# Fewer block products for the query, gate and up matmuls of an attention and feed-forward layer: q through DRAM, one unit per 64-row half

## The chip, the cores and the metric

The kernel runs on one core of one Trainium2 chip. The metric is device time in microseconds of one execution, without the launch. Four runs of the kernel before lie within 0.06% (556.2 to 556.51 us). Five engines matter here: PE (TensorE, the matrix unit; its weight loads are listed apart as PEld), DVE (VectorE), ACT (ScalarE), POOL (GpSimd) and SP (SyncE, which here does nothing but issue DMAs). In the traces here each engine works through its own queue in the order in which the program put the instructions there; when the q stores alone left SP's queue (e9_storepool, below), a wait of PE fell from 19.2 to 3.4 us.

## The reference, cut to what matters

```python
# x: 2048 x 448, bf16.  16 query heads of 256, 8 key/value heads, last W = 512 keys
xn = layernorm(x)
q  = xn @ wq                                    # 448 -> 16 x 256
p  = softmax(q @ k[last 512]^T * 256 ** -0.5)   # two query heads share a kv head
s  = (p @ v[last 512]) @ wo                     # 16 x 256 -> 448
g  = silu((gelu(xn @ w_gate) * (xn @ w_up)) @ w_down)   # 448 -> 1792 -> 448
out = x + s * g
```

The contraction of q, gate and up has length 448 = 7 x 64. That is an awkward length for the matmuls of 128 rows that the traces show elsewhere (128*128): three full ones and a half one.

## The kernel before

It computes on tokens in four chunks of 512. Everything between the end of the head and the tail is a queue of matmuls on PE with the other engines behind it. Two outputs of a pair, j = 0 and 1 (gate and up of 128 columns, or the two 128-column halves of a q head), are computed together: one 64-row half of PE works for one output while the other half works for the other, and then they change over (such a pair took 0.2157 us, below).

```python
def group(units, lo, hi, start, stop, phases=(0, 1)):
    for p in phases:
        ...                                     # cut: ks is [2, 1, 0, NK]; NK is the 64-row rest
        for (b, w, wr, cols, reads, rreads, xts) in units:
            for k in ks:
                if k == NK and ph == 1:
                    continue
                for u, j in ((0, ph), (1, 1 - ph)):      # the two 64-row halves, side by side
                    rows = slice(R * u, R * u + R)
                    l = wr[rows] if k == NK else w(j, k)[rows]
                    lst.append((bank[b + j][:, lo:hi], l, xnT[rows, k, cols], ...))
```

So an output costs seven 64-row matmuls of 512 columns, and a pair of outputs takes seven slots of PE. The order of work: all gate and up (112 units of 128 columns by 512 tokens), with the down projections of finished chunks between them; then attention, where q is computed for 8 or 12 heads at a time and kept in SBUF until it is used:

```python
LAG = 2
for m in range(NS):                 # 4 chunks x 16 heads
    if m in groups:                 # q for the next 8 or 12 heads
        for i in range(m, groups[groups.index(m) + 1], 2):
            q_group(i, (cur, nxt)[i // 2 % 2])
    s_mm(m)      # 8 matmuls; exp on ACT into p; DVE scales p into pn;
                 # SP issues two DMA transposes pT <- pn (dma_t)
    if len(late) == LAG:
        pv(late.pop(0))             # 8 matmuls of pT with v
    ...                             # cut: after 16 heads, 64 matmuls with wo for each 256 tokens
    late.append(m)
```

All weights, keys and values lie in SBUF before attention starts: wq, kT, va and wo are loaded from POOL's and SP's queues in the middle of gate and up, when nobody is waiting for them.

The softmax here doesn't subtract the row's maximum and nothing guards it: scores larger than these inputs give would overflow.

Of the kernel before, what the change touches and what calls it, by code (L numbers as in the profile page):

```python
# [8 lines left out]
F32 = mybir.dt.float32  # L9

LN_EPS = 1e-5
P = 128
# [3 lines left out]
class Buf:  # L16
# [3 lines left out]
    __slots__ = ("lo", "hi", "writer", "readers")  # L20

    def __init__(self, lo, hi):
        self.lo, self.hi = lo, hi
        self.writer = None
        self.readers = []

# [10 lines left out]
class Plan:  # L37
# [16 lines left out]
    def buf(self, lo=0, size=0):  # L54
        b = Buf(lo, lo + size)
        self.bufs.append(b)
        return b

    def reuse(self, new):


        for b in new:
            for x in self.bufs:
                if x not in new and x.lo < b.hi and b.lo < x.hi:
                    b.readers.extend(x.readers)
                    if x.writer is not None:
                        b.readers.append(x.writer)

    def op(self, eng, fn, reads=(), writes=(), dma=False, after=()):
        o = Op(eng, fn, dma)  # L70
        raw = {b.writer: None for b in reads if b.writer is not None}
        deps = dict(raw)
        for b in writes:
            if b.writer is not None:
                deps[b.writer] = None
            deps.update((x, None) for x in b.readers)


        for d in deps:
            if d.eng == eng and not d.dma and not dma and (eng == "pe" or d not in raw):  # L80
                continue
            o.deps.append(d)
        o.deps.extend(after)
        for b in writes:
            b.writer, b.readers = o, []
        for b in reads:
            b.readers.append(o)
        self.ops.append(o)
        return o
# [75 lines left out]
def bass_recurrent_scan__sliding_block_cached__geglu_ffn__prompt_kernel(  # L165
# [19 lines left out]
    QC = 512  # L185
# [12 lines left out]
    HG = 8  # L198
    NG = Hq // HG
    QS = 12  # L200

    es = ExitStack()
    with es:
# [3 lines left out]
        def place(name, shape, dt, at=None):  # L207
            size = {BF16: 2, F32: 4}[dt]
# [36 lines left out]
        xnT, a, _ = place("xnT", [P, NK + 1, S], BF16)  # L245
        b_xnT = [[K.buf(), K.buf()] for t in range(NT)]
        g2, a, _ = place("g2", [P, NT, D], BF16)
        b_g2 = sbuf_bufs(a, D * 2, NT)
        kT, a, _ = place("kT", [P, Hkv, 2, W], BF16)
        b_kT = sbuf_bufs(a, 2 * W * 2, Hkv)  # L250
        va, a, _ = place("va", [P, Hkv, NJ, Dh], BF16)
        b_va = [K.buf() for g in range(Hkv)]
        wq, a, _ = place("wq", [P, NK, HD], BF16)
        wqr, a, _ = place("wqr", [P, Hq, P], BF16)
        b_wql = [[K.buf() for i in range(3)] for g in range(NG)]
        NXR = 3
        xr, a, _ = place("xr", [P, NXR, D], BF16)
        b_xr = sbuf_bufs(a, D * 2, NXR)
        ofin, a, _ = place("ofin", [P, 2, D], BF16)
        b_ofin = [[K.buf(a + (i * D + lo) * 2, (hi - lo) * 2) for lo, hi in ((0, CUT), (CUT, D))] for i in range(2)]  # L260
# [3 lines left out]
        rw = base[0]  # L264
        wo, _, rw_end = place("wo", [P, NCO, D], BF16)
        b_wo = sbuf_bufs(rw, 8 * D * 2, NCO // 8)
        x4, a, a2 = place("x4", [P, NT, D], BF16, at=rw)
        b_x4 = sbuf_bufs(a, D * 2, NT)
        NXN = (rw_end - a2) // (DP * 2)
        xn, a, a2 = place("xn", [P, NXN, DP], BF16, at=a2)  # L270
        b_xn = [[K.buf(a + i * DP * 2, D * 2), K.buf(a + i * DP * 2 + D * 2, R * 2)] for i in range(NXN)]
        assert a2 <= rw_end

        rf = base[0]
        wgu, a, at = place("wgu", [P, 2, NK, F], BF16, at=rf)
        wgur, _, at = place("wgur", [P, F], BF16, at=at)
        b_wgu = K.buf(a, at - a)
        FBL = [0, 3, 6, 9, NF]
        b_wl = [[K.buf() for j in range(2)] for i in range(4)]
        b_wlr = [[K.buf() for j in range(2)] for i in range(3)]  # L280
        wd, a, at = place("wd", [P, NF, D], BF16, at=at)
        b_wd = K.buf(a, at - a)
        actT, a, at = place("actT", [P, 2, NF, QC], BF16, at=at)
        b_actT = [sbuf_bufs(a + i * NF * QC * 2, QC * 2, NF) for i in range(2)]
        NGL = 3
        gl, a, at = place("gl", [P, NGL, QC], BF16, at=at)
        b_gl = sbuf_bufs(a, QC * 2, NGL)


        NPT, NPN, NP32 = 3, 3, 3  # L290
        pT, a, at = place("pT", [P, NPT, 2, 2, NJ, P], BF16, at=rf)
        b_pT = [sbuf_bufs(a + i * QC * NJ * 2, QC * NJ, 2) for i in range(NPT)]
        pn, a, at = place("pn", [P, NPN, 2, W], BF16, at=at)
        b_pn = sbuf_bufs(a, 2 * W * 2, NPN)
        p32, a, at = place("p32", [P, NP32, W], F32, at=at)
        b_p32 = sbuf_bufs(a, W * 4, NP32)
        assert at <= b_wgu.hi
        oT, a, at = place("oT", [P, NCO, QC], BF16, at=b_wgu.hi)
        b_oT = sbuf_bufs(a, QC * 2, NCO)
        qT, a, at = place("qT", [P, QS, 2, QC], BF16, at=b_gl[0].lo - (QS - HG) * 2 * QC * 2)  # L300
        assert b_oT[-1].hi <= a
        b_qT = [[K.buf(a + (h * 2 + e) * QC * 2, QC * 2) for e in range(2)] for h in range(QS)]
# [8 lines left out]
        def qs(n):  # L311
            return QS - 1 - n % QS


# [6 lines left out]
        def act(o, i, func, reads, writes, scale=1.0):  # L321
            K.op("act", lambda e, o=o, i=i: e.activation(o, i, func, scale=scale), reads, writes)  # L322
# [167 lines left out]
        def gu_evac(n, b):  # L490
            c, f = divmod(n, NF)
            s = n % NGL
            act(gl[:, s, :], bank[b], ACT.Gelu_apprx_tanh, (b_ps[b],), (b_gl[s],))
            K.op("dve", lambda e: e.tensor_tensor(actT[:, c % 2, f, :], bank[b + 1], gl[:, s, :], ALU.mult),  # L494
                 (b_ps[b + 1], b_gl[s]), (b_actT[c % 2][f],))

        def down(c, pairs):
            for t4 in range(4):
                t = c * 4 + t4
                b = bk(pairs, t4)  # L500
                mms([(bank[b][:, 0:D], actT[:, c % 2, f, t4 * P:(t4 + 1) * P], wd[:, f, :], f == 0, f == NF - 1)
                     for f in range(NF)], [b_wd] + b_actT[c % 2], (b_ps[b],))
                s = t % 2
                act(tmp[:, s, :], bank[b][:, 0:D], ACT.Tanh, (b_ps[b],), b_tmp[s], scale=0.5)
                K.op("dve", lambda e, t=t, b=b, s=s: e.scalar_tensor_tensor(
                    out=g2[:, t, :], in0=tmp[:, s, :], scalar=1.0, in1=bank[b][:, 0:D],
                    op0=ALU.add, op1=ALU.mult), b_tmp[s] + [b_ps[b]], (b_g2[t],))
# [61 lines left out]
        def load_k(g):  # L569
            dma_t(kT[:, g, :, :], A_k_cache[0, g, Sk - W:Sk, :], (), (b_kT[g],))  # L570

        def load_v(g):
            dma("pool", va[:, g, :, :],
                A_v_cache[0, g, Sk - W:Sk, :].rearrange("(j p) d -> p j d", p=P), (), (b_va[g],))

        def load_wq(g):
            lo, hi = g * HG * Dh, (g + 1) * HG * Dh
            dma("pool", wq[:, :, lo:hi], A_wq[0:K3, lo:hi].rearrange("(k p) f -> p k f", p=P), (), (b_wql[g][0],))
            for e in range(2):
                dma("pool", wqr[R * e:R * e + R, g * HG:(g + 1) * HG, :],  # L580
                    A_wq[K3:D, lo:hi].rearrange("p (h e f) -> p h e f", e=2, f=P)[:, :, e, :], (), (b_wql[g][1 + e],))

        DOWN_AT = {NF + 5: 0, 2 * NF + 1: 1}
# [4 lines left out]
        NU = NQC * NF  # L588
        cur, nxt = (0, 2), (4, 6)
        for n in range(4, NU, 2):  # L590
# [4 lines left out]
            if ln_t[0] < 8 or n >= 12:  # L595
# [6 lines left out]
            if n == 32:  # L602
                for g in range(NG):
                    load_wq(g)
                for g in range(Hkv):
                    load_v(g)
                for g in range(Hkv):
                    load_k(g)
                K.reuse(b_wo)
                for i in range(NCO // 8):  # L610
                    dma("pool", wo[:, i * 8:(i + 1) * 8, :],
                        A_wo.rearrange("(c p) d -> p c d", p=P)[:, i * 8:(i + 1) * 8, :], (), (b_wo[i],))
                for t in range(NXR):
                    dma("pool", xr[:, t, :], x_view[:, t, :], (), (b_xr[t],))
            if n + 1 in DOWN_AT:
                down(DOWN_AT[n + 1], cur)
                cur, nxt = nxt, cur


        def q_group(n, pairs):  # L620

            c, h = divmod(n, Hq)
            units = [(b, lambda j, k, i=i: wq[:, k, (h + i) * Dh + j * P:(h + i) * Dh + (j + 1) * P],
                      wqr[:, h + i, :], slice(c * QC, (c + 1) * QC), b_wql[h // HG][:1], b_wql[h // HG][1:], b_xnT[c * 4:c * 4 + 4])
                     for i, b in enumerate(pairs)]
            group(units, 0, QC, True, True)
            for i, b in enumerate(pairs):
                s = qs(n + i)
                act(qT[:, s, 0, :], bank[b], ACT.Copy, (b_ps[b],), (b_qT[s][0],))
                K.op("dve", lambda v, s=s, b=b: v.tensor_copy(qT[:, s, 1, :], bank[b + 1]),  # L630
                     (b_ps[b + 1],), (b_qT[s][1],))

# [161 lines left out]
```

## Time and profile before

| | before |
|---|---|
| time, median of 3 runs | 556.32 us (556.2 to 556.45) |
| span of the profiled run | 554.7 us, granted PE clock 1.00 |
| PE busy | 547.6 us, 99% |
| read from and written to HBM | 17.92 MB, 1.84 MB |

The page's first part gives busy time by engine, the fourth the chain of work that ended last, the fifth the costliest groups of instructions (busy time, mean ns of one, then the idle time before them and who ended it), the sixth the DMAs with the time from issue to landing. Of the kernel before:

```profile
PE 547.6 (99%) x3603; PEld 261.2 (47%) x3628; DVE 317.2 (57%) x817; ACT 273.6 (49%) x727; POOL 32.7 (6%) x64
...
PEclk9999999999999999999999999999999999999999
...
PE 98%; DMA 1%; issue 0%; DVE 0%; SPq 0%; ACT 0%
...
L328 PE MATMUL bank<-xnT,wq 64*128 64x512 bf16 x768 | 94.4, 376 | 0.0
L328 PEld LDWEIGHTS bank<-xnT,wq 64*128 64x128 bf16 x768 | 36.9, 94 | 46.5 <-ACT p L643 2.1
...
L647 DVE TENSOR_SCALAR pn<-p,rden 128x512 bf16<-128x512 f32 x256 | 124.6, 487 | 14.4 <-DMA pT<-pn 5.4
...
pT<-pn SPq DMA_TRANSPOSE x128, 2.8
```

PE is the bound: 98% of the chain is PE's own work, and the weight load of 94 ns is hidden behind the matmul that runs (a slot is 216 ns, below). The row PEclk shows full clock in all 40 slices. PE's list of waits is nearly empty (total us, times, longest us):

```profile
PE bank L445 <- DVE epst L359: 1.2, 1, 1.2
PE bank L328 <- ACT qT L322: 1.0, 6, 0.2
...
```

What a slot costs is read from PE's timeline in gate and up (start, length, and how many matmuls stand in the piece):

```profile
53.71 2.11 PE L328 MATMUL bank<-xnT,wgu 64*128 64x512 bf16 x18
55.65 0.38 PE L328 MATMUL bank<-xnT,wgur 64*128 64x512 bf16 x2
55.87 0.81 PE L328 MATMUL bank<-xnT,wgu 64*128 64x512 bf16 x6
56.52 0.38 PE L328 MATMUL bank<-xnT,wgur 64*128 64x512 bf16 x2
56.73 0.38 PE L328 MATMUL bank<-xnT,wgu 64*128 64x512 bf16 x2
```

From 53.71 to 56.73 there are 28 matmuls, 14 pairs: 0.2157 us for a pair of half-array matmuls. A matmul's own length of 0.38 us is not its cost, because matmuls overlap (the first piece ends at 55.82, the next has begun at 55.65); only the distance between starts counts. With this slot, the stages can be added up from counts: gate and up 84.6 us, down 42.3, q 96.6, scores and values 220.9, output projection 96.6, head and tail about 13: 554 us, which is the span.

One stage has another engine near its limit. In a stretch of score and value matmuls, the sixteen DMA engines are 0.87 busy (last two numbers: granted clock, then DMA share, then GB/s):

```profile
core 0: us, PE busy (x) PEld busy (x) DVE busy (x) ACT busy (x) POOL busy (x), PEclk, DMA share, GB/s
201.00:212.00 11.00, 10.89 (x51) 5.00 (x51) 9.05 (x28) 9.03 (x28) 0.00 (x0) 1.00 0.87 160
```

### The profile page before, as it was taken

To read this page: it belongs to the slowest core of one execution; us is meant where nothing else is said; L and a number is where in the kernel's file an instruction comes from. 1 tells how busy PE (TensorE), PEld (TensorE's weight loads), DVE (VectorE), ACT (ScalarE), POOL (GpSimd) and SP (SyncE) were. 2 spreads that over 40 slices of the span, in tenths; PEclk is the share of its full clock that TensorE was granted. 3 is DMA by queue.
4 is the path that set the end of the run, shared out by engine and by line. 5 is a ranking of instruction groups with operands and counts; after the bars stand their busy time and mean duration, and the time that the engine had idled before them with its cause. 6 is when DMAs were issued, how large, how long until landed. Compare 5 with 4: busy or idle time off the path is not lost.

```text
span 554.7 us, 9719 instructions
## 1 busy us (share of the span) xinstructions
PE 547.6 (99%) x3603; PEld 261.2 (47%) x3628; DVE 317.2 (57%) x817; ACT 273.6 (49%) x727; POOL 32.7 (6%) x64
## 2 busy tenths in 40 slices
PE   8999999999999999999999999999999999999997
PEld 5554444444544444554444444544444454444455
DVE  6673734443385588326588745258747625858722
ACT  5432324353485588205588635058747505758600
POOL 1120580000000000000000000000000000000000
PEclk9999999999999999999999999999999999999999
DMA  9540399901156077413086803157704713618601
GB/s 295 115 141 9 79 302 307 213 1 39 38 134 96 5 149 157 88 35 92 1 153 152 153 1 77 33 94 164 146 11 95 134 34 90 153 19 153 153 8 34
DMA packets 163599, 57.63 MB, mean 104 GB/s; under 512 B 151456, under 2 KB 160672, under 8 KB 163552
## 3 DMA queue, kind: packets, MB, share of 16 engines
q1 hardware_dynamic: 159488, 45.16, 38.8%
q0 software_dynamic: 3296, 11.27, 6.7%
q8 instruction: 29, 0.48, 0.4%
q10 hardware_dynamic: 768, 0.57, 0.3%
q14 instruction: 18, 0.15, 0.1%
HBM read 17.92 MB, written 1.84 MB: 36 GB/s over the span
## 4 chain that ended last, share of the span: by engine, by line
PE 98%; DMA 1%; issue 0%; DVE 0%; SPq 0%; ACT 0%
PE bank L328 98%; DMA x<-in_A_x_dram 1%; SPq L316 0%; DVE stats L375 0%; ACT xnT L322 0%; DVE tmp L681 0%; ACT ve L391 0%; DVE ofin L684 0%; PE bank L426 0%; DVE mv L378 0%
## 5 line engine op out<-in xcount | busy, mean ns | idle before, releaser
L643 ACT ACTIVATE p<-bank 128x512 f32<-128x512 f32 x256 | 149.2, 597 | 103.3 <-PE bank L328 101.4
L647 DVE TENSOR_SCALAR pn<-p,rden 128x512 bf16<-128x512 f32 x256 | 124.6, 487 | 14.4 <-DMA pT<-pn 5.4
L328 PE MATMUL bank<-pT,va 128*128 128x512 bf16 x512 | 120.8, 379 | 0.0
L328 PE MATMUL bank<-kT,qT 128*128 128x512 bf16 x487 | 117.8, 379 | 2.0 <-ACT qT L322 1.0
L328 PE MATMUL bank<-wo,oT 128*128 128x448 bf16 (+2 forms) x544 | 97.7, 341 | 0.0
L328 PE MATMUL bank<-xnT,wq 64*128 64x512 bf16 x768 | 94.4, 376 | 0.0
L328 PE MATMUL bank<-xnT,wgu 64*128 64x512 bf16 (+2 forms) x768 | 83.9, 350 | 0.4 <-ACT xnT L322 0.4
L328 PEld LDWEIGHTS bank<-pT,va 128*128 128x128 bf16 x512 | 50.1, 98 | 60.4 <-DMA pT<-pn 0.2
L328 PEld LDWEIGHTS bank<-kT,qT 128*128 128x128 bf16 x512 | 49.6, 98 | 61.3 <-issue 2.5
L328 PEld LDWEIGHTS bank<-wo,oT 128*128 128x128 bf16 x544 | 52.0, 98 | 45.5
L630 DVE CAST qT<-bank 128x512 bf16<-128x512 f32 x64 | 42.9, 692 | 51.9 <-PE bank L328 51.9
L322 ACT ACTIVATE qT<-bank 128x512 bf16<-128x512 f32 x64 | 38.2, 597 | 60.7 <-PE bank L328 59.1
L328 PEld LDWEIGHTS bank<-xnT,wq 64*128 64x128 bf16 x768 | 36.9, 94 | 46.5 <-ACT p L643 2.1
L322 ACT ACTIVATE gl<-bank 128x512 bf16<-128x512 f32 x56 | 33.2, 597 | 49.4 <-PE bank L328 46.2
L494 DVE TENSOR_TENSOR actT<-bank,gl 128x512 bf16<-128x512 f32 x56 | 37.8, 689 | 33.4 <-PE bank L328 26.6
L328 PEld LDWEIGHTS bank<-xnT,wgu 64*128 64x128 bf16 x768 | 36.9, 94 | 37.4 <-issue 0.7
L643 ACT ACTIVATION_READ_ACCUMULATOR p<-bank 128x1 f32 x256 | 52.8, 206 | 0.0
L646 DVE RECIPROCAL rden<-rsum 128x1 f32<-128x1 f32 x256 | 40.4, 158 | 20.6 <-ACT p L643 20.0
L681 DVE SCALAR_TENSOR_TENSOR tmp<-bank,g 128x448 f32<-128x448 f32 (+2 forms) x17 | 10.1, 597 | 72.5 <-PE bank L328 72.5
L666 DVE CAST oT<-bank 128x512 bf16<-128x512 f32 x64 | 43.8, 684 | 6.9 <-PE bank L328 6.9
L328 PE MATMUL bank<-wd,actT 128*128 128x448 bf16 x224 | 43.0, 353 | 0.0
L322 ACT ACTIVATE oT<-bank 128x512 bf16<-128x512 f32 x64 | 39.1, 611 | 7.0 <-PE bank L328 7.0
(39 smaller groups left out, 182.9 us busy)
## 6 DMA issues: line engine op xcount, KB each, us to landing
wo<-in_A_wo_dram POOLq DMA_DIRECT2D x4, 896.0 KB, 19.0
wq<-in_A_wq_dram POOLq DMA_DIRECT2D x2, 1536.0 KB, 10.0
va<-in_A_v_cache_dram POOLq DMA_DIRECT2D x8, 256.0 KB, 13.9
pT<-pn SPq DMA_TRANSPOSE x128, 2.8
xr<-in_A_x_dram POOLq DMA_DIRECT2D x16, 112.0 KB, 2.3
out_dram<-ofin SPq DMA_DIRECT2D x15, 112.0 KB, 1.7
wd<-in_B_w_down_dram SPq DMA_DIRECT2D x1, 1568.0 KB, 7.6
x<-in_A_x_dram SPq DMA_DIRECT2D x2, 448.0 KB, 4.4
```

The lines of the kernel that those rows point to most:

```text
L322: K.op("act", lambda e, o=o, i=i: e.activation(o, i, func, scale=scale), reads, writes)
L328: ins = e.matmul(o, lhsT=l, rhs=r, start=st, stop=sp)
L494: K.op("dve", lambda e: e.tensor_tensor(actT[:, c % 2, f, :], bank[b + 1], gl[:, s, :], ALU.mult), (b_ps[b + 1], b_gl[s]), (b_actT[c % 2][ ...
L630: K.op("dve", lambda v, s=s, b=b: v.tensor_copy(qT[:, s, 1, :], bank[b + 1]), (b_ps[b + 1],), (b_qT[s][1],))
L643: K.op("act", lambda e, b=b, r=r, z=z: e.activation(p32[:, z, :], bank[b], ACT.Exp, scale=att_scale, accum_out=rsum[:, r:r + 1]), (b_ps[b] ...
L646: K.op("dve", lambda e, r=r: e.reciprocal(rden[:, r:r + 1], rsum[:, r:r + 1]), (b_rsum[r],), (b_rden[r],))
L647: K.op("dve", lambda e, r=r, z=z, y=y, t=t4 % 2: e.tensor_scalar(pn[:, y, t, :], p32[:, z, :], rden[:, r:r + 1], None, op0=ALU.mult), (b_p ...
L666: K.op("dve", lambda v, i=i, b=b: v.tensor_copy(oT[:, i, :], bank[b]), (b_ps[b],), (b_oT[i],))
L681: K.op("dve", lambda e: e.scalar_tensor_tensor(out=tmp[:, s, c0:c1], in0=bank[b][:, c0:c1], scalar=0.5, in1=g2[:, t, c0:c1], op0=ALU.mult, ...
```

## The change

The intent is to do less on PE. A product of 2 x 2 blocks normally needs eight block products; the well-known trick of Strassen and Winograd does it with seven, for the price of sums of blocks before and after. Here the four output blocks are two outputs by two token chunks, and the contraction of 384 rows is split into two parts of 3 x 64; the last 64 rows are handled apart. A set of four output blocks costs 7 x 3 + 4 = 25 half-array matmuls where it cost 28. The form is used for all of q and for half of gate and up: 23 jobs of two sets, one set on each 64-row half of PE. (The first half of gate and up stays plain: the "plain stage" below. The stage of the 23 jobs, with nine down tiles between them, is the "product stage".)

```python
# 25 matmuls per half; * has 4-byte operands
"P1" 3, "P6"* 3, "P5"* 3, "P3"* 3, "P2" 3, "P7"* 3, "P4"* 3, L12, L11, L22, "Ld"*
```

What had to be added for it, cut from the diff:

```diff
+        def xf_ops(p):        # sums of token blocks, on POOL, results 4 bytes wide
+                    (1.16, lambda ...: pool_tt(x[:, 0, k, :], y, z, ALU.add, ...)),   # and 3 more, and a cast
+        def w_ops(i, js):     # sums of weight blocks, on POOL: 6 operations for a job's set
+        def load_wu(i, kind, n):      # 12 DMAs of 64 x 3 x 128 or smaller for gate/up, 6 for q
+                        dma("sp", dst, src, (), ...)
+        xnO[o, :, cs] <- xnT[i, 0:NK, cs]        # a copy of xn with its halves exchanged, by DMA
...
+        def q_sink(n, p):     # q does not stay in SBUF
+                    stores[m] = task("sp", 0.1, 2.5, lambda: dma("sp", qd[m], qo[:, O[i].i, :, :]...
...
+                ready = [task("sp", 0.8, 4.0, lambda ...: load_wu(WU.i, kind, n), base - 3 * PER, (), [WU])]
+        for g in range(Hkv):          # keys and values only after the last use of xf[1]
+            task("sp", 0.2, 3.0, lambda g=g: dma("sp", va[:, g, :, :], ...), ..., last_p1)
+            task("sp", 0.2, 3.0, lambda g=g: dma_t(kT[:, g, :, :], ...), ..., last_p1)
+        run_schedule(pools, {"pe": 0.0, "act": 1.0, "dve": 1.5, "pool": 2.0, "sp": 0.0})
...
-        LAG = 2
+        LAG = 3
+        for i in range(NCO // 8):     # wo only now: its memory was xnT's and xnO's
+            dma("pool", wo[:, i * 8:(i + 1) * 8, :], ...)
         for m in range(NS):
             s_mm(m)
+            load_q("pool", m + QS)    # 256 KB from DRAM, 8 heads ahead
```

The order in which each engine gets its instructions in the product stage comes from a small scheduler in the kernel itself (`run_schedule`), which plays the stage with assumed durations (the first number of each `task` in the diff, in us). And because in the kernel's layout the 4-byte sums lie where keys and values go, and xnT and xnO where wo goes, keys, values and wo can be loaded only when the product stage ends, and q has to go out to DRAM and come back.

## The prediction

> **What bounds the kernel now.** TensorE. The page's busy row has PE at 99% of a 554.7 us span at clock 1.00; the chain of waits is 98% PE. In the timeline two 64x512 matmuls on the two 64-row halves run side by side, a pair in 0.2157 us (14 pairs, 53.71 to 56.73); a 128x512 matmul takes the same, a 128x448 one 0.189 (128 in 24.2). Sum: gate and up 392 pairs, 84.6; down 224, 42.3; q 448 pairs, 96.6; scores and values 1024, 220.9; output projection 512, 96.6; with 10 us of head and 3 of tail 554, the span. Only PE work or PE waits move it.
>
> **Removed.** 28 half-array matmuls (two outputs x two token chunks x seven 64-row pieces) become 25: seven products of three, and four for the last 64 rows; for half of gate and up (196 pairs) and all q (448): 644 pairs become 575. At 0.2157 us that is 14.9 us, all on the critical path.
>
> **Added.**
> 1. 16 of the 25 have 4-byte operands. The bf16 weight load takes 94 ns (by-form groups) and hides. [...] no trace here shows a 4-byte load. The new kernel's scheduler counts 0.227 us per such slot, so I expect a load just at the limit: 11 ns x 23 x 16 slots, 4 us back. Matmuls I expect at 216 ns, one pass.
> 2. Per gate/up job (two units, 5.4 to 5.6 us of PE) 10 ACT operations at about 0.53 = 5.3 us and 8 DVE at 0.69 = 5.5 us: full, with down tiles as slack; q jobs about 75%. POOL makes the weight sums; its wide work isn't in the trace. Expected PE waits 2 us (at most 5), most in the first seven jobs.
> 3. DMA: q makes 16.8 MB out and in. In score/value stretches DMA is already 0.87 busy (windows, 201 to 212) from two pT transposes per head of 3.45 us. A q load is 128 rows of 2 KB; the trace's 2048-byte packets take 86 ns, so 0.7 us of all 16 engines[...]: 3.7 us per head against 3.45. Lag 3 gives pT one head more, but pn has three buffers. The 3.7 MB wo load now falls on attention's start. Expected PE waits 1 us (at most 5).
>
> Attention's PE work is unchanged and ACT needs about 2.9 of 3.45 us per head: it stays PE-bound.
>
> **Sum.** 556.3 - 14.9 + 4 + 2 + 1 = 548.4. Predicted 548 us, range 541.5 to 558. Faster by over 2%: 0.27, within 2%: 0.63, slower by over 2%: 0.10.
>
> **What would show it.** 23 jobs of two units, 5.4 to 5.6 us each; the 4-byte load near 200 ns[...]; PE idle in all under 10 us, released by ACT, DVE or POOL in the fast stage and pT or pn in attention; pT landing at 3 to 5 us, not 2.8; heads still 3.45 us apart.
>
> **What would make it wrong.** [...] A 4-byte matmul of more than one pass. POOL far slower than planned. DMA saturating so that heads take 3.7 us (over 10 us lost). Or hidden loads and no stalls: 541.

The cuts are statements that no trace or run of this case shows. No term of the sum is among them: it came to 556.3 - 14.9 + 4 + 2 + 1 = 548.4. The 4 us are the author's estimate, from the 0.227 us that the new kernel's scheduler assumes for a slot with a 4-byte load, less the measured 0.2157.

## The result and the profile after

| | before | after |
|---|---|---|
| time, median of 4 runs each | 556.38 us | 615.48 us |
| lowest to highest | 556.2 to 556.51 | 615.17 to 616.34 |
| span of the profiled run | 554.7 us, clock 1.00 | 613.4 us, clock 0.969 |
| PE busy | 547.6 us, 99% | 560.8 us, 91% |
| HBM read, written | 17.92, 1.84 MB | 38.83, 18.61 MB |

The changed kernel is slower: ratio 1.1065, 95% interval 1.105 to 1.1081. A ratio here and below is the mean time of one kernel's fast runs over that of the other's of the same rounds, so it is not quite the ratio of the medians quoted beside it. The outputs were judged correct.

The page after:

```profile
PE 560.8 (91%) x3490; PEld 318.3 (52%) x3518; DVE 359.8 (59%) x882; ACT 335.0 (55%) x847; POOL 161.5 (26%) x227
...
PEclk9998969999999999589899999999999999999999
...
PE 64%; DMA 14%; SPq 7%; DVE 6%; POOL 3%; ACT 3%; issue 2%; DVEq 0%; ACTq 0%; POOLq 0%
...
L746 PE MATMUL bank<-xf,wf 64*128 64x512 f32 x690 | 144.7, 453 | 28.5 <-DVE qo L770 19.2
L1178 DVE TENSOR_SCALAR pn<-p,rden 128x512 bf16<-128x512 f32 x256 | 124.7, 487 | 60.5 <-DMA pT<-pn 53.1
L746 PEld LDWEIGHTS bank<-xf,wf 64*128 64x128 f32 x690 | 108.0, 192 | 43.7 <-DVE qo L770 21.7
...
wu<-in_A_wq_dram SPq DMA_DIRECT2D x40, 96.0 KB, 2.6
...
pT<-pn SPq DMA_TRANSPOSE x128, 3.9
```

There are fewer matmuls, as intended, and the chain is no longer PE's: 14% of it is DMA and 7% the SP queue. PE's clock dips in four places. PE's waits, the long ones:

```profile
PE bank L746 <- DVE qo L770: 19.2, 5, 13.4
PE bank L385 <- ACT p L1174: 8.9, 7, 5.6
PE bank L385 <- DVE actT L551: 8.7, 6, 4.1
PE bank L746 <- POOL xf L629: 6.3, 2, 4.3
```

Each of these belongs to one stage, and one table sorts the loss by stage. The borders are PE's first and last matmuls of a kind in the two timelines (after the change the product stage begins at 72.4 us, and attention at 271.2 with the first score matmul); the middle row of the kernel before adds up the same work from its counts, because there it was done at several places.

| stage | before, us | after, us | difference |
|---|---|---|---|
| head, plain gate and up, down of the first chunk | 61.1 | 72.4 | +11 |
| the work of the product stage: half of gate and up, q, nine down tiles | 42.3 + 96.6 + 23.9 = 162.8 | 198.8 | +36 |
| attention, three down tiles, output projection, tail | 330.8 | 342.2 | +11 |

The sum, 58.7 us, is the difference of the spans. The expected gain of 14.9 us should have been found in the middle row; it lies 51 us above 162.8 - 14.9 = 147.9.

**The plain stage.** PE waits six times for DVE, the longest time in the down projection, and DVE meanwhile waits for POOL. From PE's timeline and from DVE's:

```profile
50.38 3.17 PE L385 MATMUL bank<-wd,actT 128*128 128x448 bf16 x8 [4.08 <-DVE actT L551]
```

```profile
48.38 0.61 DVE L458 TENSOR_SCALAR xn<-x,mv,rstd 128x448 bf16<-128x448 bf16 x2 [6.47 <-POOL rstd L444]
```

The layernorm of the later tokens needs rstd from POOL. On POOL's queue, before this rstd (47.70), stand sums of weight blocks (43.33 to 47.40), the first of which waited 3.49 us for weights that were still being loaded. On DVE's queue the finished gate and up results (actT, 49.65) stand behind that layernorm, so they wait too. The starts of PE's matmuls show 9.6 us lost in six gaps.

**The product stage.** Its first jobs wait 2.4 and 5.1 us for the sums of tokens on POOL. Its last job waits longest. PE's timeline, then SP's queue at that moment:

```profile
245.51 0.39 PE L746 MATMUL bank<-xf,wf 64*128 64x512 f32 x1
259.35 0.79 PE L746 MATMUL bank<-xf,wf 64*128 64x512 f32 x1 [13.45 <-DVE qo L770]
```

```profile
236.02 1.34 SPq L376 DMA_TRANSPOSE kT<-in_A_k_cache_dram  x1
237.41 0.57 SPq L373 DMA_DIRECT2D va<-in_A_v_cache_dram  x1
...
251.63 0.45 SPq L373 DMA_DIRECT2D q_all<-qo  x1
252.13 1.51 SPq L376 DMA_TRANSPOSE kT<-in_A_k_cache_dram  x1
...
254.36 6.48 SPq L373 DMA_DIRECT2D q_all<-qo  x6
```

This is one chain: PE needs a bank that DVE must empty into a qo buffer; every qo buffer still waits to be stored; the stores stand on SP's queue behind eight key transposes of at least 1.2 us and eight value loads of 0.52 to 0.58. The scheduler had planned 0.2 us for each load and 0.1 for a store. In the same way SP's queue holds back the weight sets in the gate and up jobs: a set is twelve DMAs at 0.65 us from one to the next, 7.8 us of issuing for a job that needs about 5.7 us of PE (planned: 0.8).

```profile
107.15 1.90 SPq L373 DMA_DIRECT2D wu<-in_B_w_gate_dram  x3
...
111.10 1.90 SPq L373 DMA_DIRECT2D wu<-in_B_w_gate_dram  x3
```

The issue is not small beside the DMA itself: 0.61 us of SP's queue (median) for a 48 KB load that takes 2.3 us (median) from issue to landing, and it held these jobs back, as e5_nowu tests below.

These waits also cost clock. The record of the granted clock shows half clock (0.50) in four stretches: 3.41 us from 50.4, 10.24 from 77.7, 17.07 from 248.3 and 6.83 from 289.3, and full clock between them. Each began during or right after one of the long waits (in the timeline 4.08 us to 50.38, 2.01 to 77.67, 13.45 to 259.35 and 5.59 to 290.56), and was partly spent in it. In them the matmuls of one 64-row half start 0.43 us apart (84.88, 85.31, 85.74), where after them it is 0.22 (88.13, 88.36, 88.57). Shorter waits did not do it: five of 0.48 to 1.43 us between 29 and 43 us left the clock at 1.00. How long a wait must be is not shown.

**Attention.** After the first stretch the PE waits are short, but the DMA engines are full. A pT transpose held SP's queue for 1.24 us (median), and for up to 7.69 in the first heads, with a DMA share of 1.02 (273 to 288 us); before the change 2.44 was the most. The windows of the product stage (its border here lies after the scores of the first head), of the first stretch of attention, and of a later one:

```profile
72.40:272.60 200.20, 170.34 (x1304) 133.68 (x1313) 114.57 (x167) 119.52 (x223) 98.46 (x111) 0.93 0.48 147
272.60:349.60 77.00, 70.24 (x311) 30.18 (x315) 51.61 (x164) 56.28 (x171) 14.01 (x24) 0.96 1.06 236
455.00:512.00 57.00, 55.38 (x253) 24.70 (x256) 44.61 (x140) 45.65 (x142) 9.44 (x17) 1.00 1.04 207
```

The DMA share (last but one) is 1.06 where wo and q are loaded together; it adds up the times of packets, so a figure above 1 means that some of them overlapped. The first stretch, up to the first output projection, takes 76.9 us where its matmuls need 66.6 (three down tiles 7.9, scores of 18 heads 31.1, values of 16 heads 27.6; the texts count the first head's scores too and say 68.3). Of the 10.3 us between, 6.5 are gaps, and by an estimate 2.8 are half clock, in which 5.6 us of PE's work fell (289.3 to 296.1). Later stretches of 16 heads take 57.0 us where 256 slots need 55.2.

### The profile page after: what moved, and what is told of

The parts are those of the page before. It is cut to its first block, busy times and chain, and to the rows that moved or that the text cites. A ratio compares the mean times of both kernels' runs of the same rounds, so it can differ in the third digit from the quotient of the medians.

```text
span 613.4 us, 10384 instructions
## 1 busy us (share of the span) xinstructions
PE 560.8 (91%) x3490; PEld 318.3 (52%) x3518; DVE 359.8 (59%) x882; ACT 335.0 (55%) x847; POOL 161.5 (26%) x227
## 3 DMA queue, kind: packets, MB, share of 16 engines
HBM read 38.83 MB, written 18.61 MB: 94 GB/s over the span
## 4 chain that ended last, share of the span: by engine, by line
PE 64%; DMA 14%; SPq 7%; DVE 6%; POOL 3%; ACT 3%; issue 2%; DVEq 0%; ACTq 0%; POOLq 0%
PE bank L385 47%; PE bank L746 16%; DMA pT<-pn 10%; SPq L373 5%; DVE pn L1178 2%; DMA q_all<-qo 2%; SPq L376 2%; POOL xf L629 2%; DMA wu<-in_B_w_up_dram 1%; PE bank L502 1%; DVE qo L770 1%; ACT p L1174 1%; POOL wf L629 1%; DMA xnO<-xnT 1%; DVE actT L551 1%
## 5 line engine op out<-in xcount | busy, mean ns | idle before, releaser
L746 PE MATMUL bank<-xf,wf 64*128 64x512 f32 x690 | 144.7, 453 | 28.5 <-DVE qo L770 19.2
L1178 DVE TENSOR_SCALAR pn<-p,rden 128x512 bf16<-128x512 f32 x256 | 124.7, 487 | 60.5 <-DMA pT<-pn 53.1
L385 PE MATMUL bank<-kT,qT 128*128 128x512 bf16 x491 | 121.9, 382 | 10.2 <-ACT p L1174 8.9
L746 PEld LDWEIGHTS bank<-xf,wf 64*128 64x128 f32 x690 | 108.0, 192 | 43.7 <-DVE qo L770 21.7
L385 PEld LDWEIGHTS bank<-kT,qT 128*128 128x128 bf16 x512 | 48.4, 98 | 73.8 <-ACT p L1174 19.8
L373 POOL DMA_DIRECT2D qT<-q_all x58 | 33.0, 568 | 189.9 <-PE bank L385 163.6
L746 PE MATMUL bank<-xnT,wu 64*128 64x512 bf16 x276 | 70.1, 383 | 0.0
L629 POOL TENSOR_TENSOR wf<-wu 128x384 fp32r<-128x384 bf16 x34 | 30.9, 916 | 70.7 <-PE bank L746 57.1
L379 ACT ACTIVATE gl<-bank 128x512 bf16<-128x512 f32 x56 | 31.8, 601 | 30.8 <-PE bank L385 28.8
L385 PE MATMUL bank<-xnT,wgu 64*128 64x512 bf16 (+2 forms) x432 | 43.2, 329 | 4.7 <-DVE actT L551 4.6
L385 PE MATMUL bank<-wd,actT 128*128 128x448 bf16 x189 | 39.4, 363 | 5.2 <-DVE actT L551 4.1
L373 POOL DMA_DIRECT2D xr<-in_A_x_dram x16 | 8.7, 543 | 121.0 <-DVE ofin L1216 104.4
```

The costliest lines, as they stand in the source:

```text
L373: K.op(q, lambda e, o=o, i=i: e.dma_start(o, i), reads, writes, dma=True)
L379: K.op("act", lambda e, o=o, i=i: e.activation(o, i, func, scale=scale), reads, writes, own=own)
L385: ins = e.matmul(o, lhsT=l, rhs=r, start=st, stop=sp)
L629: K.op("pool", lambda e: e.tensor_tensor(o, x, y, op), reads, writes, own=True)
L746: o = K.op("pe", lambda e: e.matmul(bank[bi][:, 0:w_], lhsT=l, rhs=r, start=st, stop=True, skip_group_check=True), reads(), (b_ps[bi],), a ...
L1178: K.op("dve", lambda e, r=r, z=z, y=y, t=t4 % 2: e.tensor_scalar(pn[:, y, t, :], p32[:, z, :], rden[:, r:r + 1], None, op0=ALU.mult), (b_p ...
```

## The experiments

The leading theory after this reading: the loss is waiting, made by in-order queues (SP and POOL) whose DMA issues and sums take longer than planned, and by DMA traffic in attention. Rivals: the 4-byte operands themselves (slower loads or matmuls), and DMA load alone. The texts name theories by letters: A is the 4-byte slot, C the q traffic in attention, F the issuing of weight loads on SP's queue; any other letter is explained where it stands. Runs with one execution have no known state, and one version below spread over 5 us in four runs, so a difference of 2 or 3 us between single runs decides nothing: for these, the verdict rests on the lengths of stages in the traces. The kernel before, run beside each, took 556.1 to 556.8 us (medians).

A caution about correctness: the output is x plus a small term, and the check of the outputs passed even for runs that were made wrong. It says nothing about the accuracy of sums in two bytes.

### e1_bf16: the sums in 2 bytes, everything else in place

```diff
-            t, a, at = at_(off, name, [P, 5, NK, QC], F32R)
+            t, a, at = at_(off, name, [P, 5, NK, QC], BF16)      # same addresses; the weight sums likewise
```

> The sums of the seven products (weights and rows) are kept in 2-byte instead of 4-byte form; order of instructions unchanged. Theory A (the 4-byte weight load, 183 to 198 ns in the trace, sets the pace of a half: 0.236 us per slot in the cleanest stretch, 39 slots from 155.85 to 165.05, against 0.2157 before): loads fall to about 94 ns, a clean 25-slot job falls from 5.90 us to 5.4 to 5.5, and the time falls by 5 to 12 us (603 to 610; less than 23 x 0.5 if waits take it back). Rival B (the pace is set by evictions and by two independent streams in one in-order queue): the clean job stays at 5.8 to 6.0 us and the time within 2 us of 615.5. Accuracy may be lost.

Measured: 610.56 us against 615.48. The load of the summed weights becomes 96 ns:

```profile
L750 PEld LDWEIGHTS bank<-xf,wf 64*128 64x128 bf16 x690 | 50.3, 96 | 80.6 <-DVE qo L774 24.0 <-POOL xf L633 9.2 <-issue 5.4
```

A job is 50 half-array matmuls, 25 slots. Take the time of every 50 successive matmuls with no down tile among them: a quarter of these times lie below 5.708 us in the changed kernel and below 5.395 in e1_bf16, which is 0.2158 us per slot. So 4-byte operands cost 0.31 us a job, 7.2 us in 23 jobs, where 4 had been predicted; that is 20 ns in each of the 16 slots with 4-byte operands, where 11 had been predicted. The run narrowed the weights and the rows that pass through them together, so it does not show which of the two costs this time. The 4-byte matmul did not take twice as long: the cleanest stretch before this run has 0.236 us per slot. Theory A is real but small: 54 us of the loss remain. The total lies just above the 603 to 610 us that A had been given.

### e2_kv: only the first two key/value pairs at the end of the product stage

```diff
-        for g in range(Hkv):
+        for g in range(2):                    # the other six: one pair before every second head
```

> Only keys and values of head pairs 0 and 1 are loaded at the end of the product stage; the other six pairs are loaded inside attention, two pairs ahead. Theory: q stores queued behind eight key transposes (1.23 us of issue each) and value loads on the SP queue hold the q tiles, and PE then waits 13.8 us (245.5 to 259.4) and loses clock: that wait goes, the time falls by 12 to 18 us, to 597 to 604. Rival (the stores wait for their own data or for DMA bandwidth, not for the queue's order): the wait stays over 8 us and the time within 4 us of 615.5.

Measured: 613.55 us. The long wait is gone, as PE's waits show, and the last matmul of the product stage comes 17 us earlier (253.5 us in place of 270.7), as expected. But the total, for which 597 to 604 us had been expected, hardly moves:

```profile
PE bank L385 <- ACT p L1174: 20.4, 15, 7.9
...
PE bank L746 <- DVE qo L770: 6.1, 5, 1.6
```

The wait for qo fell from 19.2 to 6.1 us; the wait for p in attention rose from 8.9 to 20.4. The first stretch of attention takes 91 us in place of 77, with DMA shares of 1.00 to 1.16. The loads still have to be done at a moment when the DMA engines are full. The wait was moved, not removed.

### e3_noq: no q loads in attention (wrong)

```diff
             s_mm(m)
-            load_q("pool", m + QS)            # the first 8 heads' q is used throughout
```

> Wrong on purpose: after the first eight heads no q is loaded in attention, and the old eight are used again. Theory C (q loads on top of 0.87 busy DMA engines slow the pT transposes, so pn waits): the three later 16-head stretches of scores and values take 55.2 us instead of 57.0, pT lands in 2.8 us instead of 3.9, and the time falls by 4 to 10 us, to 605 to 611. Rival D (the 8.6 us lost at attention's start are the wo load and the start of the pipeline, and lag or buffers limit the rest): the first stretch (272.7 to 349.6) keeps its loss, and the time falls by under 4 us.

Measured: 605.12 us, 10 us less. A later stretch of attention, where the changed kernel has a DMA share of 1.04:

```profile
447.00:502.00 55.00, 55.00 (x256) 24.95 (x255) 45.87 (x142) 46.61 (x144) 0.54 (x1) 1.00 0.82 146
```

Later stretches now take 55.4 us in place of 57.0, and pT lands after a median of 3.2 us in place of 3.9. C holds: attention takes 334.1 us in place of 342.2, so q's way back through DRAM is worth about 8 us there. The other 2 us of the total lie earlier, before any q load that is left out, and a single run cannot tell them from none. The first stretch, 71.9 us, is still 5.3 above its matmuls.

### e4_order: weight loads and sums only after the last layernorm step

```diff
-            if n in (10, 12, 14):
-                load_wu(n // 2 - 5, "gu", n // 2 - 5)
-            if n == 18:
+            if n == 16:
+                assert ln_t == [NT, NT]
                 for c in (2, 3): load_xnO(c)
+                load_wu(0, "gu", 0)
+                pending += w_ops(0, [0] * 6) + [o for d, o in xf_ops(1)]   # sets 1 and 2 at n = 18, 20
```

> In the plain gate and up stage the weight loads and POOL's weight sums are issued after the last layer-norm step, and the row sums before the second set of weight sums; nothing else. Theory E (POOL's queue holds the reciprocal deviation of late tiles behind weight sums that wait for their loads, so DVE, then PE wait; and the row sums are late): the stretch up to the last plain gate/up matmul falls from 72.4 us to 63 to 65, the wait of 7 us for the first row sums at 75 to 83 falls below 3, and the time falls by 8 to 16 us, to 599 to 607. Rival (plain stage is slow for other reasons[...]): 72.4 stays above 69 and the time within 5 us of 615.5.

Measured: 612.35 us. The plain stage ends at 66.6 us in place of 72.4, so the theory of rstd behind the sums holds for 6 of its 11 us. Yet the waits for the token sums (2.7 and 5.1 us) remain, and of the 6 us only 3 reach the end, which a single run cannot tell from none. The total decides nothing here; the stage does.

### e5_nowu: four weight sets of gate and up not loaded (wrong)

```diff
+            if kind == "gu" and n >= 3:
+                return                        # the jobs use whatever lies in the buffer
```

> Wrong on purpose: four of the seven gate/up weight sets of the product stage are not loaded (old weights are used). Theory F (in the gate/up jobs the SP queue is the limit: twelve loads a set at 0.65 us of issue each are 7.8 us, where the schedule counts 0.8): the stretch of four jobs and two down tiles from 96.7 to 126.5, 29.8 us, falls to 26 to 28, and the time by 3 to 6 us, to 609 to 612. Rival G (ACT, DVE and POOL set these jobs): the stretch stays within 1 us of 29.8.

Measured: 615.06 us, no change in total. In the stretch of gate and up jobs between two down tiles (about 94 us to 127 us after the start) the time falls from 33.0 to 29.2 us, so issuing these loads does hold those jobs back, as F says. But the q jobs after it give it back: one stretch of them takes 23.8 us in place of 21.9. What one wait releases, the next one takes, as long as the stores of q set the pace behind it.

### e6_compact: 2-byte sums, and keys and values loaded early into the room this frees

```diff
-            at = a + 5 * NK * QC * 4                # the room that e1 left empty
+        kT, a, at = at_(o_xf1 + 16 * KB, "kT", [P, Hkv, 2, W], BF16)
-            task("sp", 0.2, 3.0, ... va ..., last_p1); task("sp", 0.2, 3.0, ... kT ..., last_p1)
+            task("sp", 1.25, 4.5, ... kT ..., one pair per job from job 9 on)   # and va with 0.6
```

> Two-byte sums as in e1_bf16 take half the room; keys and values get the other half and are loaded during the q jobs, one head pair per job, instead of all at the end. Theory: the 13 us wait at the end of the product stage goes, as in e2_kv, and this time the start of attention is not burdened instead: against e1_bf16 (610.6) the time falls by 14 to 24 us, to 587 to 597. Rival (the DMA engines are short all over the second half, so that the wait turns up elsewhere again, as it did in e2_kv): over 603.

Measured: 601.44 us, 9 us below e1_bf16; 14 to 24 had been expected, so this was a miss. The wait at the end is gone and the product stage is 13.5 us shorter than e1_bf16's (last product matmul at 253 us). But the plain stage is 1.3 us longer, and attention 3, with a wait of 6.9 us for p in a first stretch of about 79 us (e1_bf16: 77.6). Once more a part of the gain is lost at the start of attention.

### e7_late: as e6_compact, with wo in four parts after heads 5, 8, 11 and 14

```diff
-        for i in range(NCO // 8): dma("pool", wo[:, i * 8:(i + 1) * 8, :], ...)   # before attention
+            if m in (5, 8, 11, 14):
+                i = m // 3 - 1
+                dma("pool", wo[:, i * 8:(i + 1) * 8, :], ...)
```

> e6_compact with the output weights (3.7 MB) loaded in four parts after heads 5, 8, 11 and 14 instead of at once at the start of attention. Theory C (DMA engines are overfull at attention's start): the first 19 heads, up to the first projection block, take 3 to 8 us less than in e6_compact, and the time falls by as much. Rival D (start of the pipeline, not DMA): no change within 1.5 us.

Measured: 621.36 us, 20 us more than e6_compact, the opposite of what was expected. The first stretch takes about 100 us, with twelve waits for p, 21.9 us in all and up to 3.9. Putting the load later did not put it where the DMA engines are free. My reading, which no run tests by itself, is that in the first heads PE has other work (scores and down tiles) while transposes are slow, and later has none.

### e8_order: e7_late with the order of e4, two of five token sums first, casts on ACT

```diff
+                pending += w_ops(0, [0] * 6) + [xo[5 * k + j] for k in range(NK) for j in (0, 1)]
+                pending += [lambda k=k: xo[5 * k + 4]("act") for k in range(NK)] + ...
```

> e7_late with the changed order of loads and sums of e4_order, and the row sums of the first two products made first, copies on ACT. Theory E: product stage starts without the waits of 4 and 5 us for row sums and without the half clock after them; against e7_late 9 to 15 us less. Rival: DVE, which does two layer-norm steps per two units, limits the plain stage, and the row sums only come when it is done: 4 to 6 us less, as e4_order alone gave 3.1.

Measured: 621.29 us, the same as e7_late. The plain stage ends at 66.5 us, the product stage starts with one wait of 2.3 us and ends at about 250; so neither the gain of 9 to 15 us nor the rival's 4 to 6 reached the total. The first stretch of attention then takes 100 us. The early gain is real and again swallowed whole by attention's start.

### e9_storepool: q stores on POOL's queue

```diff
-                    stores[m] = task("sp", 0.1, 2.5, lambda: dma("sp", qd[m], ...
+                    stores[m] = task("pool", 0.6, 3.0, lambda: dma("pool", qd[m], ...
```

> Changed kernel with the 64 q stores issued from the POOL queue instead of the SP queue; nothing else is moved. Theory H (q tiles are held because their stores stand behind weight loads, 0.65 us of issue each, and key transposes, 1.23 us each, on the in-order SP queue): the waits of PE for DVE's q tiles (19.2 us in all, 13.4 the longest) fall below 6, the end of the product stage comes at 250 to 257 instead of 271. The total falls by 5 to 18 us (597 to 610), less than that if attention's start stretches, as in e2_kv. Rival (the stores are slow in themselves): waits stay over 12 us.

Measured: 607.02 us, 8.5 us less than the changed kernel. This is the cleanest test of SP's queue: no DMA is taken away, only the stores no longer stand behind the loads.

```profile
PE bank L385 <- ACT p L1174: 17.0, 8, 12.3
...
PE bank L746 <- DVE qo L770: 3.4, 5, 1.5
```

The wait for qo falls from 19.2 to 3.4 us, the median job from 6.42 to 5.72, the product stage's last matmul from 270.7 to 252.7 us; all three figures that had been expected were met. So SP's in-order queue is shown as the cause of 16 of these 19 us; and about half of them come back as one long wait for p at the start of attention.

### e10_nowo: changed kernel with wo set to zero by POOL, not loaded (wrong)

```diff
-            dma("pool", wo[:, i * 8:(i + 1) * 8, :], ...)
+            K.op("pool", lambda e, i=i: e.memset(wo[:, i * 8:(i + 1) * 8, :], 0.0), (), (b_wo[i],))
```

> Wrong on purpose: changed kernel with the output weights zeroed by POOL instead of loaded. Theory C (DMA engines are overfull at attention's start; wo is 14 us of their time by the estimate from its packets): the stretch from the first to the end of the third last down tile to the first projection block, 76.9 us from 272.7 to 349.6, falls to 70 to 73, pT's longest landing from 12.7 us to under 8; the time falls by 4 to 7 us. Rival D: stretch and time unchanged within 1.5 us.

Measured: 617.71 us. The experiment made its own wait, so it decides nothing on wo. DVE's timeline while POOL zeroes:

```profile
275.90 7.83 DVE L1178 TENSOR_SCALAR pn<-p,rden 128x512 bf16<-128x512 f32 x1
...
283.84 0.49 DVE L1178 TENSOR_SCALAR pn<-p,rden 128x512 bf16<-128x512 f32 x1
```

POOL's four memsets took 3.1 us each, one after the other from 271.3 to 283.4. One DVE instruction, begun during the second, ended 0.3 us after the fourth: 7.83 us in place of 0.49. So it lasted through the rest of the second memset and the whole of the third and the fourth, and did not end between two of them. Another DVE instruction, at 273.61 beside the first memset, took its usual 0.62 us. By what the memsets held the one and not the other, no run shows.

### e11_sum: the repairs together

2-byte sums, keys and values early (e6), the order of e8, stores on POOL (e9), one more qo buffer, wo at once.

```diff
-        NQO = 6
+        NQO = 7                     # the rest as in e6_compact, e8_order and e9_storepool
```

> All that helped together: two-byte sums, keys and values early, order of loads and sums of e8_order, seven instead of six q tiles, q stores from the POOL queue; the output weights at once, as in the changed kernel. If the theories add up: plain stage to 67, product stage to 240 (25-slot jobs near 5.4 to 6), attention as in e6_compact 346: 583 to 592 us, still slower than before by over 4%. If waits only move: over 597.

Measured: median 586.36 us of four runs (584.08 to 589.09), ratio to the kernel before 1.0558 (1.053 to 1.0585). This was as expected, and it is the fastest correct version with the change. The plain stage ends at 66.6 us, the product stage at 234; a job's median is 5.50 us and its best 5.395, so within a job the scheme runs nearly as designed. PE's waits:

```profile
PE bank L389 <- ACT p L1185: 13.1, 10, 9.0
PE bank L750 <- ACT su L383: 3.2, 2, 2.1
PE bank L389 <- DVE actT L555: 3.1, 4, 1.4
```

29 of 59 us are recovered. The first stretch of attention takes 80.8 us, 14.2 above its matmuls, of which 9 are one wait.

### e12_sum_noq, e13_nowo and e14_nowo_noq: what remains

All three start from e11_sum. Their outputs are wrong, which doesn't matter for the times. e12 leaves out the q loads after the first eight; e13 sets wo to zero by DVE in place of loading it; e14 does both.

```diff
-            load_q("pool", m + QS)                                   # e12, e14
-            dma("pool", wo[:, i * 8:(i + 1) * 8, :], ...)            # e13, e14
+            K.op("dve", lambda e, i=i: e.memset(wo[:, i * 8:(i + 1) * 8, :], 0.0), (), (b_wo[i],))
```

> Wrong on purpose: e11_sum without the q loads inside attention. If q through DRAM costs attention about 9 us (e3_noq), 8 to 11 us below e11_sum; the three later stretches of 16 heads at 55.2 to 55.6 us. If other things hold attention as well, under 5 us.

> Wrong on purpose: e11_sum with the output weights zeroed by DVE instead of loaded (in e10_nowo POOL did it, and DVE stood still for it, so that run decided nothing). Theory C (wo's DMA at attention's start holds the transposes): the stretch from the third last down tile to the first projection block, 80.8 us in e11_sum (235.9 to 316.7), falls to 73 to 77, and the time by 4 to 8 us. Rival D: unchanged within 1.5 us.

> Wrong on purpose: e13_nowo also without the q loads inside attention. If the two together are all that holds attention, the same stretch falls to 68 to 70 us (its PE work is 68.3), the later ones stay at 55.2 to 55.6, and the time is 569 to 573. If the start of the pipeline costs besides, the stretch stays over 72.

Measured: e12 576.84 us, e13 588.03, e14 573.43. Without q loads, later stretches of attention take 55.4 us, and the time falls by 9.5 from e11's median; attention itself is 8.4 us shorter, as in e3. e13's total lies inside e11's range: its first stretch is 4 us shorter, but the zeroing itself makes a wait of 6.0 us there, and its later stretches happened to be longer (59.7 and 60.4), so as a single test it missed. With both loads away, the first stretch is 75.2 us, above the 72 that had been expected, with one wait of 5.6 us, which the zeroing makes (DVE's four memsets of 1.55 us each, 237.3 to 244.5). Without that wait it is 69.6 against 66.6 of matmuls; by an estimate 2.7 of the 3 us left are half clock after the wait, in which 5.4 us of PE's work fell (244.5 to 251.3; fourteen 128x448 matmuls took 5.08 us there). PE waits for p nowhere else:

```profile
PE bank L389 <- ACT p L1185: 5.6, 1, 5.6
```

So q's loads and wo's load together explain attention's loss. What is left in e14 is instructive. Its product stage, from 66.9 to 234.2, takes 167.4 us (e11's 167.7); the old form of the same work takes 162.8. With 69 slots saved and most of the long waits repaired, the new form is still not shorter than the old. But e14 is not the form's limit: eight gaps over 0.6 us are left in this stage, 9.6 us in all, and after single waits of 2.3 and 2.5 us half clock began at 73.8 and 101.1 (the clock of the whole run is 0.985); by an estimate, half of two stretches of 3.4 us, this is another 3.4 us. Without both it would be about 154 us; no run reached that.

### e15_before_q: the kernel before with a 256 KB DRAM-to-DRAM copy per head (correct)

```diff
             s_mm(m)
+            dma("pool", q_like[m],
+                A_k_cache[0, m % Hkv, Sk - W:Sk, :].rearrange("(p a) d -> p (a d)", a=4),
+                (), b_qT[qs(m)])
```

> The kernel before, plus one 256 KB DMA per head in attention, paced as the q loads are, from DRAM to DRAM: the DMA work of q through DRAM alone, with lag 2, results unchanged. Theory C: pT lands later than 2.8 us and PE waits in the score/value stretches; 3 to 12 us slower than before. Rival: no change beyond 1 us, and the cost in the changed kernel comes from something else in its attention.

Measured: median 578.94 us of four runs (578.32 to 582.02), ratio 1.0418 (1.0388 to 1.0448): 22 us slower, where 3 to 12 had been expected. The stretch that was at 0.87, and PE's waits:

```profile
201.00:212.00 11.00, 9.79 (x45) 4.10 (x44) 7.66 (x24) 8.10 (x26) 1.49 (x3) 1.00 1.02 210
```

```profile
PE bank L329 <- DMA pT<-pn: 17.8, 23, 1.4
```

The clock stayed full and PE's list names no new wait but this one: traffic alone is enough to make attention wait for pT, whose landing goes from 2.8 to 4.2 us. As a size it does not carry over to q's loads without more: this copy's packets take 1.06 us of all sixteen engines per head, and a q load in the changed kernel 1.03, so the traffic is about the same; but its packets are of 16 KB and not 4, and the lag here is 2, not 3.

## Why the prediction was wrong

- **The bound was read correctly.** PE was the bound, a slot is 0.2157 us, and the removal was right: 25 slots in place of 28 were run, and e1_bf16's best jobs take 25 x 0.2158 us.
- **The 4-byte load** ("11 ns x 23 x 16 slots, 4 us back"). The direction was right: the load took 192 ns on average against 94, close to the limit of the slot, and the matmul did not take twice as long. The size was 7.2 us (e1_bf16), 20 ns a slot and not 11; whether the load alone makes it is not shown, as e1_bf16 narrowed the rows too. Why a 4-byte load takes twice as long is not shown.
- **The step that failed is item 2: "Expected PE waits 2 us (at most 5), most in the first seven jobs."** The starts of PE's matmuls show 32.7 us of gaps over 0.6 us each in the product stage alone. The prediction compared busy time per job on ACT and DVE and found it just enough. It did not cost the in-order queues of SP, whose issuing shows in no busy row, and of POOL, which is only 26% busy. The trace of the kernel before already had the numbers. A transpose (pT) occupies SP's queue for 1.26 us there (median), and the first plain loads from SP look like this:

```profile
1.18 0.42 SPq L316 DMA_DIRECT2D wgu<-in_B_w_gate_dram  x1
1.65 0.48 SPq L316 DMA_DIRECT2D x<-in_A_x_dram  x1
2.17 0.56 SPq L316 DMA_DIRECT2D wgur<-in_B_w_gate_dram  x1
```

  With 0.4 to 0.6 us each, twelve loads per job were never to be had for the 0.8 us that the scheduler assumed. e9_storepool shows that 16 us of PE waits vanish when only the stores leave that queue; e5_nowu shows the weight loads at work in the gate and up jobs.
- **The plain stage was not costed at all.** It was taken to be as before and lost 11 us, 9.6 of it in waits for DVE. Moving the new loads and sums behind the last layernorm step gave 6 back (e4_order).
- **The half clock was not costed.** All four stretches of it began during or right after long waits. In the product stage PE worked about 5 us (82.8 to 87.9) and 6 us (259.4 to 265.4) at half speed (0.43 us between starts in place of 0.22); by an estimate from these, that added half of it, about 5.5 us. The 3.4 us from 50.4 in the plain stage added another 1.7, and the 5.6 us of work at the start of attention 2.8: about 10 us in all.
- **Adding up the product stage**: 51 us above the ideal are 7.2 (4-byte slots), 32.7 (gaps), about 5.5 (clock); the remaining 5.5 or so lie in gaps under 0.6 us that were not followed one by one.
- **Item 3, "Expected PE waits 1 us (at most 5)" in attention.** The traffic argument was right in direction: with the q loads the DMA share of later stretches is 1.00 to 1.06 where it is 0.82 to 0.84 without them (e3_noq), and pT lands after 3.9 us. A q load was mis-sized: predicted at 0.7 us of all DMA engines per head, its 64 packets of 4 KB took 1.03 (257 ns each on average). The conclusion was too mild: attention lost 11 us. About 8 went when the q loads were left out (e3_noq, and e12 against e11). The rest is at its start, a wait of 3.9 us and half clock; with wo's load gone too (e14_nowo_noq), PE waited for p only where the zeroing made it wait. The text had named pn's three buffers as a limit of the longer lag; DVE waited 53.1 us for transposes to free pn buffers, as the groups show, so three pn buffers had no slack. The effect of the lag alone was not tried.
- **The margin was thin from the start.** Repairs of the waits alone could not have brought the full 14.9 us. Even with 2-byte slots, the whole gain is 69 slots, while the product form added sums on POOL, copies and additions on ACT and DVE, and DMA streams (weights in small pieces, q out and in, wo late) to a kernel whose PE was 99% busy. The best correct version lost 5.6%, and e14 shows the product stage itself at 167.4 us against 162.8, with about 13 us of waits and half clock still in it.

What stays open: the small gaps of the product stage, the lag of 3 and the number of pn buffers. That each half of PE runs as a unit of its own costs nothing in e1_bf16's best jobs (0.2158 us per slot). The mechanism of wo's load was shown by its removal together with q's, not by itself, since zeroing the memory made a wait of its own. No experiment beat the kernel before.

## What to carry to other kernels

When a change takes work off a PE that is already 99% busy, list for each new DMA which queue issues it, how long the issue takes in a trace, and what stands behind it; a queue of DMA issues shows up in no busy row, yet it set the pace here (16 of 19.2 us of waits went when the stores left SP's queue). A wait that is removed upstream is worth only what the next resource has free (in e2_kv 13.1 us less of waits for qo, 11.5 more for p), so follow the gain to the end of the program before counting it. And memory is part of the cost: the room that the sums and the second copy of xn took in SBUF forced q out to DRAM and wo into the stage where the DMA engines were already 0.87 busy.
